# Attention ahead of two MLPs: one of four chunks of p·v as three rounded matmuls, heads 4 to 37

## Chip, cores and metric

One core of one Trainium2 chip. The metric is the device time of one launch in microseconds. The kernel before took 1683.31 us (median of 3 runs, 1678.78 to 1685.2).

## What is computed

Attention over 4 batches of 12 heads (448 tokens, 64 features each), with an RMS norm of q and k ahead of it; then an MLP block with a layer norm; then a second MLP block behind a low-rank mix along the tokens. All of it is 32-bit. The change touches the last product of the attention alone:

```python
q_n, k_n = (rmsnorm(q, g_q), rmsnorm(k, g_k))
scores = scale * np.matmul(q_n, k_n.transpose(0, 1, 3, 2))
scores = scores - np.max(scores, axis=-1, keepdims=True)
attn = np.exp(scores)
attn = attn / (np.sum(attn, axis=-1, keepdims=True) + 1e-09)
return np.matmul(attn, v)
```

## The kernel before

The 48 heads run as a software pipeline; the keys of a head are cut into NC = 4 chunks of CP = 112. In stage i of the loop over heads six generators take turns, one step each per chunk, in the order of `OS`: `sc` (scores of head i and their exp), `mx` (row maxima, head i+2), `pv` (p times v, head i-1), `t1` (transposes of k and q, head i+3), `t2` (transposes of the query's low part, head i+1), `norm` (copying out, head i-2). A stage has four such steps. Beside them run background generators: `pre` (norm of a pair of heads and its split into high and low parts), `pre_v` (load of v for a pair of heads), and from head 14 on the layer norm of the batch that is done (`ln_stats`, `ln_apply`), which works on batch 0 behind head 14 and on batch 1 behind head 26.

What stands in 32 bits is multiplied in two ways. Nearly all products are made from a rounded high part and a low part (type `F32R`, three matmuls). The product p·v alone uses 32-bit operands (`F32`):

```python
if c < NX:
    PE.matmul(po[:, :S], vf[:, j, c, :], ps[c], start=(c == 0), stop=(c == NC - 1))
```

NX is 4, so all chunks go this way, and the branch with `ph, pl` is not used. `vf` holds v in 64 of 128 columns; the others are ones, so that row 64 of the result is the sum of the exponentials.

The order on each engine comes from a scheduler that moves instructions by its own estimate, save those that are pinned to the order of the program. Each engine runs its queue strictly in that order. Names for the steps below: on ScalarE (ACT) L479 is the exp, L303 and L306 round k and q in `pre`, L439 copies the transposed q (`bq`) out of PSUM, L406 issues the load of v. On GpSimd (POOL) L300 scales k and q, L305 and L308 take their low parts, L287 multiplies with the gains, L184 and L219 belong to the layer norm. On VectorE (DVE) L450 takes the maxima and L514 copies the result out. On TensorE (PE) L475 and L476 make the scores, L449 the scores for the maxima, L428, L436 and L463 transpose, L500 is p·v. Seven PSUM banks go round among all these.

Of the kernel before, what the change touches and what calls it, by code (L numbers as in the profile page):

```python
# [8 lines left out]
F32 = mybir.dt.float32  # L9
F32R = mybir.dt.float32r  # L10
# [3 lines left out]
AF = mybir.ActivationFunctionType  # L14
ALU = mybir.AluOpType
AX = mybir.AxisListType

B, H, S, D = 4, 12, 448, 64
P = 128
CP = 112  # L20
NC = S // CP
DM = H * D
DFF = 4 * DM
KD = DM // P
# [6 lines left out]
NWF = 5  # L31
NP0 = 2
EPS = 1e-6
NX = 4
OS = "smpabn"
QW = D + 2
HL = 8
PVY = (0, 1, 2)
# [5 lines left out]
def f32(ap):  # L44
    return ap.bitcast(F32)


def build(tc, qkv, gg, g_ln, w1a, w2a, w1b, w2b, u_in, v_in, out):
    nc = tc.nc
    V, A, PL, PE = nc.vector, nc.scalar, nc.gpsimd, nc.tensor  # L50
    with ExitStack() as es:
# [9 lines left out]
        def bank(name, tag=None):  # L61
            cnt[0] += 1
            tag = tag or banks["tag"]
            return banks["pool"].tile([P, 512], F32, tag=tag, name=f"{name}{cnt[0]}", bufs=banks[tag])
# [40 lines left out]
        v4 = const([4 * R, S], F32R, "v4")  # L105

        def load_ggt(tp):
            gsb = tp.tile([CP, 2, D], F32, tag="gsb", name="gsb")
            nc.scalar.dma_start(gsb, gg)
            ggt = tp.tile([CP, D], F32, tag="ggt", name="ggt")  # L110
            V.scalar_tensor_tensor(ggt, gsb[:, 0, :], 1.0 / D ** 0.5, gsb[:, 1, :], ALU.mult, ALU.mult)
            return ggt
# [29 lines left out]
        def pin(ins):  # L142
            return tc.keep_in_program_order(ins) if pins[0] else ins
# [82 lines left out]
        def attention(ap, ep, ep2, early, late):  # L226
            NH = B * H
            NP = NH // 2
            kks, vfs, vhs, vls, a2s = [], [], [], [], []
            st = {}  # L230
# [13 lines left out]
            pre_load(0)  # L244
            side["ln"] = bank("ln", "ln")
            ggt = load_ggt(ap)
            identr = ap.tile([CP, CP], F32R, tag="identr", name="identr")
            pin(V.tensor_copy(identr, ident[:CP, :CP]))
# [2 lines left out]
                PE.matmul(warm[:, :P], ones_m, ones_m, start=True, stop=True)  # L251
            later = ap.tile([CP, D], F32, tag="later", name="later")
            for i in range(2):
                for lst, nm, dt, one in ((vfs, "vf", F32, 1.0), (vhs, "vh", F32R, 1.0), (vls, "vl", F32R, 0.0)):
                    n = NX if nm == "vf" else NC - NX
                    if n == 0:
                        lst.append(None)
                        continue
                    t = ap.tile([CP, 2, n, P], dt, tag=f"{nm}{i}", name=f"{nm}{i}")
                    PL.memset(f32(t[:, :, :, D:P]), one)  # L260
                    lst.append(t)
            for i in range(NA2):
                t = ap.tile([P, S], F32R, tag=f"a2{i}", name=f"a2{i}")
                PL.memset(f32(t[D:QW, :]), 1.0)
                a2s.append(t)
            qls = []
            for i in range(3):
                t = ep.tile([CP, 2 * NC, QW], F32R, tag=f"ql{i}", name=f"ql{i}")
# [133 lines left out]
            def pre_v(pr):  # L402
                b, hp = divmod(pr, H // 2)
                v = qkv[b, hp, :, 2].rearrange("p (j c) d -> p j c d", j=2)
                for j in range(2):
                    ins = (nc.scalar if pr else nc.sync).dma_start(vfs[pr % 2][:, j, :, 0:D], v[:, j, 0:NX])  # L406
                    if pr:
                        pin(ins)
                if NX == NC:
                    return  # L410
                vr = ap.tile([CP, 2, NC - NX, D], F32, tag="vr", name=f"vr{pr}", bufs=2)
                nc.sync.dma_start(vr, v[:, :, NX:])
                yield
                yield
                yield
                vh, vl = vhs[pr % 2], vls[pr % 2]
                for j in range(2):
                    A.copy(vh[:, j, :, 0:D], vr[:, j])
                yield
                for j in range(2):  # L420
                    PL.tensor_tensor(vl[:, j, :, 0:D], vr[:, j], f32(vh[:, j, :, 0:D]), ALU.subtract)

            def t1(n):
                pr, j = divmod(n, 2)
# [43 lines left out]
            def sc(n):  # L468
                a1, bq, a2 = st.pop(("ab", n))
                t = st.pop(("t2", n))  # L470
                st["p", n] = ps = []
                for c in range(NC):
                    pb = bank("ps")
                    cs = slice(c * CP, (c + 1) * CP)
                    PE.matmul(pb[:CP, :S], a1[:, cs], bq, start=True, stop=False)  # L475
                    PE.matmul(pb[:CP, :S], a2[:QW, cs], t[:QW], start=False, stop=True)  # L476
                    if c < NX:
                        p = ap.tile([CP, S], F32, tag="pf", name=f"p{n}_{c}", bufs=NX + 2)
                        A.activation(p, pb[:CP, :S], AF.Exp)  # L479
                        ps.append(p)  # L480
                    else:
                        p = ap.tile([CP, S], F32, tag="p", name=f"p{n}_{c}", bufs=2)
                        ph = ap.tile([CP, S], F32R, tag="ph", name=f"ph{n}_{c}", bufs=NC - NX + 1)
                        pl = ap.tile([CP, S], F32R, tag="pl", name=f"pl{n}_{c}", bufs=NC - NX + 1)
                        A.activation(p, pb[:CP, :S], AF.Exp)
                        V.tensor_copy(ph, p)
                        PL.tensor_tensor(pl, p, f32(ph), ALU.subtract)
                        ps.append((ph, pl))
                    if c < NC - 1:
                        yield  # L490

            def pv(n):
                pr, j = divmod(n, 2)
                ps = st.pop(("p", n))
                vf, vh, vl = vfs[pr % 2], vhs[pr % 2], vls[pr % 2]
                po = bank("po")
                st["po", n] = po
                for c in range(NC):
                    if c < NX:
                        PE.matmul(po[:, :S], vf[:, j, c, :], ps[c], start=(c == 0), stop=(c == NC - 1))  # L500
                    else:
                        ph, pl = ps[c]
                        PE.matmul(po[:, :S], vh[:, j, c - NX, :], ph, start=(c == 0), stop=False)
                        PE.matmul(po[:, :S], vl[:, j, c - NX, :], ph, start=False, stop=False)
                        PE.matmul(po[:, :S], vh[:, j, c - NX, :], pl, start=False, stop=(c == NC - 1))
                    if c in PVY:
                        yield

            def norm(n):
# [52 lines left out]
            def ORD(i):  # L562
                fs = {"s": (sc, i), "m": (mx, i + MX), "p": (pv, i - 1), "a": (t1, i + T1), "b": (t2, i + T2), "n": (norm, i - NL)}
                return [fs[z] for z in OS]

            for i in range(-3 - T1, NH + 2):
                def ok(n):
                    return 0 <= n < NH
                if i == -3 - T1:
                    start = first_two()  # L570
# [13 lines left out]
                if i - 2 in (H, 2 * H, 3 * H):  # L584
                    b = (i - 2) // H - 1
# [29 lines left out]
        bufs, held, rings, ready = {}, {}, {}, {}  # L615
# [890 lines left out]
```

## Time and profile before

| what | value |
|---|---|
| median of 3 runs | 1683.31 us |
| the profiled execution, its own time | 1675.09 us |
| its span, first to last instruction | 1673.3 us |
| mean granted TensorE clock | 0.997 |
| busy: PE, DVE, ACT, POOL | 99%, 72%, 60%, 63% |
| attention's p·v (L500), first to last start | 28.5 to 338.3 us |

The attention fills the first 340 us, the MLPs the rest. Shares of busy time are means over both. A matmul's duration in the profile runs from its issue to its modelled end and overlaps the ones beside it; what a matmul costs in a row of others is read from the chain of waits, which has one piece behind the other.

### The profile page before, as it was taken

The numbers are of one execution on the slowest core, as the hardware profiler recorded it, in microseconds if no ns is written. First come the engines' busy times: TensorE is split into PE (matmuls) and PEld (weight loads), VectorE is DVE, ScalarE is ACT, GpSimd is POOL, SyncE is SP. The second block draws the span as 40 slices with busy tenths as digits, with TensorE's granted clock in tenths as the row PEclk, the third lists the DMA queues.
The fourth block names the chain that finished last, engine by engine and source line by source line (L and its number), as shares of the span: only waits on it lengthen the run. The fifth ranks groups of instructions, "written<-read, shape, count | busy, mean of one in ns | idle before, by whom it ended". The sixth has DMA issues, their size and how long they took to land.

```text
span 1673.3 us, 24654 instructions
## 1 busy us (share of the span) xinstructions
PE 1661.3 (99%) x8223; PEld 1460.3 (87%) x8223; DVE 1203.5 (72%) x1913; ACT 1000.5 (60%) x2098; POOL 1051.1 (63%) x924
## 2 busy tenths in 40 slices
PE   8999999999999999999999999999999999999999
PEld 6666666689999999999999999999999999999998
DVE  6657777879897887866767686657667854565665
ACT  7877888867878876544544455444445534454541
POOL 5446767559767787755655687555555655776752
PEclk8999999999999999999999999999999999999999
DMA  3435444766755566544445427565657463444432
GB/s 98 117 83 128 121 117 136 205 223 207 236 178 174 185 207 202 190 139 131 152 136 159 157 85 255 190 221 176 226 189 250 166 207 118 147 151 123 150 124 76
DMA packets 134430, 273.39 MB, mean 163 GB/s; under 512 B 37280, under 2 KB 57664, under 8 KB 134304
## 3 DMA queue, kind: packets, MB, share of 16 engines
q1 hardware_dynamic: 112252, 265.24, 49.8%
q10 hardware_dynamic: 22052, 6.59, 1.7%
q8 instruction: 65, 1.06, 0.3%
q14 instruction: 61, 0.50, 0.1%
HBM read 178.80 MB, written 81.96 MB: 156 GB/s over the span
## 4 chain that ended last, share of the span: by engine, by line
PE 94%; DVE 2%; DMA 1%; POOL 1%; issue 1%; ACT 1%; SPq 0%; POOLq 0%; DVEq 0%; ACTq 0%
PE bank L1111 35%; PE bank L1289 33%; PE po L500 7%; PE bank L1233 6%; PE ps L475 2%; PE b L1111 2%; PE pm L449 2%; PE ps L476 2%; PE b L1233 2%; PE t L978 1%; PE pk L428 1%; PE pq L436 1%; PE xt L968 1%; PE pt L463 0%; DMA xl<-rs 0%
## 5 line engine op out<-in xcount | busy, mean ns | idle before, releaser
L1289 PE MATMUL bank<-h,w 128*128 128x448 f32 x2655 | 586.1, 366 | 0.0
L1289 PEld LDWEIGHTS bank<-h,w 128*128 128x128 f32 x2655 | 498.3, 188 | 38.3 <-issue 0.4
L1300 DVE TENSOR_TENSOR x<-x,bank 128x448 f32<-128x448 f32 x450 | 275.8, 616 | 188.8 <-PE bank L1289 183.8
L1111 PE MATMUL bank<-xh,w 128*128 128x448 f32 x1158 | 330.5, 367 | 0.0
L785 POOL TENSOR_TENSOR w<-wf,w 128x384 fp32r<-128x384 f32 x201 | 222.7, 1119 | 133.1 <-ACT w L784 131.6
L785 POOL TENSOR_TENSOR w<-s,w 128x384 fp32r<-128x384 f32 x151 | 173.4, 1151 | 152.4 <-ACT w L784 149.1
L1111 PE MATMUL bank<-T,w 128*128 128x448 f32 x1134 | 251.9, 367 | 0.0
L1111 PEld LDWEIGHTS bank<-xh,w 128*128 128x128 f32 x1158 | 217.2, 188 | 17.5 <-issue 0.7
L1111 PEld LDWEIGHTS bank<-T,w 128*128 128x128 f32 x1134 | 212.3, 188 | 16.4
L1111 PE MATMUL bank<-xl,w 128*128 128x448 f32 x579 | 211.9, 366 | 0.0
L784 ACT CAST w<-s 128x384 fp32r<-128x384 f32 x151 | 77.1, 515 | 174.5 <-PE bank L1111 160.5
L500 PE MATMUL po<-p,vf 112*128 112x448 f32 x384 | 175.6, 539 | 0.2 <-DVE m L450 0.2
L450 DVE TENSOR_REDUCE m<-pm 112x1 f32<-112x448 f32 x192 | 118.5, 619 | 64.4 <-PE pm L449 63.8
L784 ACT CAST w<-wf 128x384 fp32r<-128x384 f32 x201 | 101.5, 514 | 100.6 <-PE bank L1111 81.7
L83 DVE SCALAR_TENSOR_TENSOR wf<-wf,raw 128x384 uint32<-128x384 uint32 x180 | 135.2, 757 | 13.2 <-ACT raw L71 5.3
L785 POOL TENSOR_TENSOR w<-raw,w 128x384 fp32r<-128x384 f32 x72 | 81.9, 1154 | 57.1 <-ACT w L784 57.0
L1111 PEld LDWEIGHTS bank<-xl,w 128*128 128x128 f32 x579 | 108.9, 188 | 8.6
L79 ACT ACTIVATE wf<-raw 128x384 f32<-128x384 f32 x180 | 99.3, 553 | 27.5 <-DMA raw<-in_w2a 11.2
L479 ACT ACTIVATE p<-ps 112x448 f32<-112x448 f32 x192 | 104.5, 546 | 4.3 <-PE ps L476 2.1
L1103 DVE SCALAR_TENSOR_TENSOR h<-tm,h 128x448 fp32r<-128x448 f32 x103 | 99.7, 968 | 2.9 <-ACT h L1102 2.2
L71 ACT ACTIVATE raw<-raw 128x384 uint32<-128x384 uint8 x180 | 100.0, 558 | 0.0
L475 PE MATMUL ps<-bq,a 128*112 128x448 f32 x192 | 98.6, 513 | 0.0
(263 smaller groups left out, 2891.1 us busy)
## 6 DMA issues: line engine op xcount, KB each, us to landing
wd<-wf SPq DMA_DIRECT2D x94, 384.0 KB
ws<-w SPq DMA_DIRECT2D x84, 384.0 KB
w<-ws SPq DMA_DIRECT2D x84, 384.0 KB
wf<-wd SPq DMA_DIRECT2D x51, 384.0 KB
raw<-wd SPq DMA_DIRECT2D x48, 384.0 KB
raw<-in_w1b SPq DMA_DIRECT2D x48, 384.0 KB
raw<-in_w2b SPq DMA_DIRECT2D x48, 384.0 KB
raw<-in_w2a SPq DMA_DIRECT2D x44, 384.0 KB
```

Source lines behind the costliest of these rows:

```text
L71: A.activation(r[:, :, 0], r.bitcast(U8).rearrange("p n (t q) -> p n t q", t=2)[:, :, 0, 3], AF.Copy, scale=1.0 / 32, bias=-31.0 / 64)
L83: V.scalar_tensor_tensor(f, f, 3, r[:, :, 0], ALU.logical_shift_left, ALU.bitwise_or)
L450: V.tensor_reduce(m[:, c:c + 1], pm[:CP, :S], AX.X, ALU.max)
L475: PE.matmul(pb[:CP, :S], a1[:, cs], bq, start=True, stop=False)
L479: A.activation(p, pb[:CP, :S], AF.Exp)
L500: PE.matmul(po[:, :S], vf[:, j, c, :], ps[c], start=(c == 0), stop=(c == NC - 1))
L784: job(A, 520, lambda: A.copy(form(key)[0], src()), ins, ("hi",) + key, [key])
L785: job(PL, 1100, lambda: PL.tensor_tensor(form(key)[1], src(), f32(form(key)[0]), ALU.subtract), [("hi",) + key], key, rel=rel)
L1111: PE.matmul(out[:, :S], wt[:, k, :], xt[:, k, :], start=(first and n == 0), stop=(last and n == 8), skip_group_check=True)
L1233: PE.matmul(at(*to)[:, :S], wt[:, e, :], xt, start=(m in "13" and n == 0), stop=(n == 2), skip_group_check=True)
L1289: PE.matmul(at(*key)[:, :S], wt[:, e % 3, :], t, start=(n == 0), stop=(n == 3 * G - 1))
L1300: V.tensor_tensor(x[b][:, e, :], x[b][:, e, :], at(*key)[:, :S], ALU.add)
```

## The change

For heads 4 to 37 the first chunk of p and of v is split into a rounded high part and a low part, and its product is three `F32R` matmuls in place of one `F32` matmul. It stands last of the four chunks in `pv`. For this VectorE rounds p (a cast), GpSimd subtracts (`part`), and once per pair of heads ScalarE rounds v and GpSimd subtracts (`pre_v`). The parts of p go into tiles that lie idle: those of the layer norm of batch 1 for heads 4 to 23, the weight ring of the MLP for heads 24 to 37. The weights of all p·v matmuls become 66 columns wide in place of 128. The gains are loaded into the last batch's `x` tile.

```diff
-NX = 4
+H0, H2, H1, NV = 4, 0, 38, 1
...
+            def parts(n):
+                return 0 if n < H0 else NV if n < H2 else 1 if n < H1 else 0
...
             def pre_v(pr):
...
+                m = parts(2 * pr)
+                if m == 0:
                     return
...
+                yield
+                yield
+                yield
+                A.copy(vh[:, :, :m, 0:D], vf[:, :, :m, 0:D])
+                yield
+                PL.tensor_tensor(vl[:, :, :m, 0:D], vf[:, :, :m, 0:D], f32(vh[:, :, :m, 0:D]), ALU.subtract)
...
+                def part(c):
+                    ph, pl = homes(n)
+                    V.tensor_copy(ph, ps[c])
+                    PL.tensor_tensor(pl, ps[c], f32(ph), ALU.subtract)
+                    hl.append((ph, pl))
+
                 for c in range(NC):
+                    if 0 <= c - 2 < parts(n):
+                        part(c - 2)
...
             def pv(n):
...
+                m = len(hl)
+                for i in range(NC):
+                    c = (i + m) % NC
+                    if c >= m:
+                        PE.matmul(po[:QW, :S], vf[:, j, c, :], ps[c], start=(i == 0), stop=(i == NC - 1))
                     else:
+                        ph, pl = hl[c]
+                        PE.matmul(po[:QW, :S], vh[:, j, c, :], ph, start=False, stop=False)
+                        PE.matmul(po[:QW, :S], vl[:, j, c, :], ph, start=False, stop=False)
+                        PE.matmul(po[:QW, :S], vh[:, j, c, :], pl, start=False, stop=(i == NC - 1))
```

All told there are 68 more matmuls (two for each of 34 heads), 34 casts on VectorE, 34 + 17 subtractions on GpSimd and 17 copies on ScalarE. The MLPs' instructions stay as they were. Line numbers of `pre` are nine higher in the changed kernel (L300 is L309 there, L305 L314, L308 L317, L287 L296, L303 L312, L281 L290), the exp is L494, `bq` L445.

On PE, the end of p·v of head 4 (`po`), before and with the change; `p_0` to `p_3` are the chunks, `xh` the tile that holds the parts of p:

```order
L500 MATMUL po_953<-p_2_903,vf_349 128x448
L436 MATMUL pq_1008<-identr,qd_839 128x112 x4
L475 MATMUL ps_1018<-bq_742,a_5_699 112x448
L476 MATMUL ps_1018<-t_5_886,a_357 112x448
L449 MATMUL pm_1023<-a_7_859,bq_914 112x448
L500 MATMUL po_953<-p_3_922,vf_349 128x448
L475 MATMUL ps_1031<-bq_824,a_6_781 112x448
```

```order
L509 MATMUL po_964<-p_3_933,vf_348 66x448
L442 MATMUL pq_1021<-identr,qd_847 128x112 x4
L491 MATMUL ps_1032<-bq_749,a_5_706 112x448
L492 MATMUL ps_1032<-t_5_895,a_364 112x448
L455 MATMUL pm_1037<-a_7_868,bq_925 112x448
L512 MATMUL po_964<-xh_87,vh_350 66x448
L513 MATMUL po_964<-xh_87,vl_352 66x448
L514 MATMUL po_964<-xh_87,vh_350 66x448
L491 MATMUL ps_1048<-bq_831,a_6_788 112x448
```

The place of the fourth 32-bit matmul holds three rounded ones; nothing else moves there.

On GpSimd, within the layer norm of batch 0 (`ln_sq`, `ln_d`), before and with the change; `xl<-p` is the new subtraction for p:

```order
L305 TENSOR_TENSOR kk_2181<-raw_1_1804,kk_2181 112x8x64
L184 TENSOR_TENSOR ln_sq_2299<-x_82,ln_mu 128x448
L219 TENSOR_TENSOR ln_d_2646<-x_82,ln_mu 128x448
L308 TENSOR_TENSOR ql_359<-raw_0_1802,qd_2180 112x8x64
L287 TENSOR_TENSOR raw_0_1977<-raw_0_1977,later 112x512
L219 TENSOR_TENSOR ln_d_2552<-x_82,ln_mu 128x448
L300 TENSOR_TENSOR raw_1_1979<-raw_1_1979,sy_2094 112x512
L300 TENSOR_TENSOR raw_0_1977<-raw_0_1977,sy_2094 112x512
```

```order
L314 TENSOR_TENSOR kk_2267<-raw_1_1865,kk_2267 112x8x64
L184 TENSOR_TENSOR ln_sq_2390<-x_82,ln_mu 128x448
L483 TENSOR_TENSOR xl_89<-p_0_2273,xl_89 112x448
L219 TENSOR_TENSOR ln_d_2757<-x_82,ln_mu 128x448
L317 TENSOR_TENSOR ql_366<-raw_0_1863,qd_2266 112x8x64
L296 TENSOR_TENSOR raw_0_2048<-raw_0_2048,later 112x512
L483 TENSOR_TENSOR xl_89<-p_0_2369,xl_89 112x448
L219 TENSOR_TENSOR ln_d_2659<-x_82,ln_mu 128x448
L309 TENSOR_TENSOR raw_1_2050<-raw_1_2050,sy_2175 112x512
L309 TENSOR_TENSOR raw_0_2048<-raw_0_2048,sy_2175 112x512
```

Two subtractions now stand ahead of the scaling of k and q; a third piece, the low part of v (L427), stands four instructions above the first row shown.

On ScalarE, behind the load of v for heads 8 and 9, before and with the change:

```order
L406 DMA vf_349<-in_qkv 112x4x64 x2
L431 CAST a_10_1129<-pk_1124 128x448
L479 ACTIVATE p_1_1140<-ps_1137 112x448
L465 CAST t_8_1151<-pt_1146 66x448
L479 ACTIVATE p_2_1161<-ps_1158 112x448
L439 CAST bq_1172<-pq_1167 128x448
L281 ACTIVATE qsq_1_1175<-raw_1_996 112x512
L479 ACTIVATE p_3_1180<-ps_1177 112x448
```

```order
L416 DMA vf_348<-in_qkv 112x4x64 x2
L437 CAST a_10_1150<-pk_1145 128x448
L494 ACTIVATE p_1_1161<-ps_1158 112x448
L471 CAST t_8_1172<-pt_1167 66x448
L494 ACTIVATE p_2_1184<-ps_1181 112x448
L425 CAST vh_350<-vf_348 112x2x64
L445 CAST bq_1195<-pq_1190 128x448
L290 ACTIVATE qsq_1_1198<-raw_1_1007 112x512
L494 ACTIVATE p_3_1204<-ps_1201 112x448
```

The rounding of v, which needs the load to have landed, stands four instructions behind its issue and ahead of the copy of `bq`.

## Rows read from the trace of the kernel before

**Rows 1.** The page, busy time of each engine, with its share and instructions.
```profile
PE 1661.3 (99%) x8223; PEld 1460.3 (87%) x8223; DVE 1203.5 (72%) x1913; ACT 1000.5 (60%) x2098; POOL 1051.1 (63%) x924
```

**Rows 2.** Busy time in two stretches of 20 us; the first line names the columns.
```profile
core 0: us, PE busy (x) PEld busy (x) DVE busy (x) ACT busy (x) POOL busy (x), PEclk, DMA share, GB/s
75.00:95.00 20.00, 20.00 (x101) 14.03 (x101) 11.54 (x24) 16.09 (x38) 9.38 (x9) 1.00 0.31 77
160.00:180.00 20.00, 20.00 (x99) 13.81 (x98) 14.70 (x30) 17.35 (x43) 16.03 (x15) 1.00 0.41 104
```

**Rows 3.** The chain of waits, last step of a stage: start, length, piece.
```profile
205.76 0.21 PE ps L475
205.97 0.20 PE ps L476
206.17 0.20 PE pm L449
206.38 0.75 PE po L500 x2
```

**Rows 4.** Groups by form, PE, 0 to 700 us: count | busy us, mean ns.
```profile
L500 PE MATMUL po<-p,vf 112*128 112x448 f32 x384 | 175.6, 539 | 0.2 <-DVE m L450 0.2
L449 PE MATMUL pm<-a,bq 128*112 128x448 f32 x192 | 73.4, 383 | 3.0 <-ACT bq L439 2.3 <-DVE u L514 0.5
```

**Rows 5.** Two lines' instructions: count, minimum, median and maximum ns, starts, form.
```profile
L131 DVE CAST v<-f x1: 383/383/383, 60.4 to 60.4; 128x448 fp32r<-128x448 f32 x1
...
L215 POOL TENSOR_TENSOR xl<-ln_d,xh x12: 1127/1144/1177, 191.1 to 285.4; 128x448 fp32r<-128x448 f32 x12
```

**Rows 6.** Groups by form, ACT, 0 to 345 us.
```profile
L303 ACT CAST kk<-raw 112x512 fp32r<-112x512 f32 x22 | 13.6, 616 | 0.0
```

**Rows 7.** Timeline of POOL between layer norms: start, us, instruction [idle before].
```profile
74.19 1.28 POOL L305 TENSOR_TENSOR kk<-raw,kk 112x512 fp32r<-112x512 f32 x1 [3.45 <-ACT kk L303]
76.66 1.28 POOL L308 TENSOR_TENSOR ql<-raw,qd 112x512 fp32r<-112x512 f32 x1 [1.19 <-ACT qd L306]
...
81.58 2.04 POOL L300 TENSOR_TENSOR raw<-raw,sy 112x512 f32<-112x512 f32 x2 [2.38 <-PE pk L428]
```

**Rows 8.** Timeline of POOL in the layer norm of batch 0.
```profile
152.38 1.15 POOL L184 TENSOR_TENSOR ln_acc<-x,ln_mu 128x448 f32<-128x448 f32 x1 [1.70 <-ACT ln_mu L172]
153.48 4.47 POOL L184 TENSOR_TENSOR ln_sq<-x,ln_mu 128x448 f32<-128x448 f32 x4
...
163.81 1.15 POOL L219 TENSOR_TENSOR ln_d<-x,ln_mu 128x448 f32<-128x448 f32 x1
164.92 2.04 POOL L300 TENSOR_TENSOR raw<-raw,sy 112x512 f32<-112x512 f32 x2
...
174.67 2.04 POOL L300 TENSOR_TENSOR raw<-raw,sy 112x512 f32<-112x512 f32 x2 [0.69 <-DVE sy L149]
```

**Rows 9.** Timeline of ACT in the same layer norm.
```profile
166.17 0.61 ACT L303 CAST kk<-raw 112x512 fp32r<-112x512 f32 x1
```

**Rows 10.** Timeline of ACT around a load of v; ACTq issues it.
```profile
67.87 0.50 ACTq L406 DMA_DIRECT2D vf<-in_qkv  x1
...
70.77 0.54 ACT L479 ACTIVATE p<-ps 112x448 f32<-112x448 f32 x1
72.02 0.53 ACT L439 CAST bq<-pq 128x448 fp32r<-128x448 f32 x1 [0.70 <-PE pq L436]
```

**Rows 11.** Timeline of PE, the first matmul that needs that `bq`.
```profile
73.67 0.37 PE L449 MATMUL pm<-a,bq 128*112 128x448 f32 x1
```

**Rows 12.** The chain of waits, transfers on it: start, us to landing.
```profile
124.28 3.50 DMA xl<-rs
...
307.69 5.95 DMA wr<-in_w2a
```

**Rows 13.** Timelines of POOL and of DVE at the same moment.
```profile
221.89 2.12 POOL L308 TENSOR_TENSOR ql<-raw,qd 112x512 fp32r<-112x512 f32 x1 [0.57 <-ACT qd L306]
222.25 0.61 DVE L555 TENSOR_TENSOR x<-x,xl 128x448 f32<-128x448 f32 x1
```

More of the change, by code (lines that the diff above doesn't have):

```diff
@@ L107, in load_ggt @@
         def load_ggt(tp):
-            gsb = tp.tile([CP, 2, D], F32, tag="gsb", name="gsb")
+            gsb = x[B - 1][:CP, 0, :2 * D].rearrange("p (j d) -> p j d", j=2)
             nc.scalar.dma_start(gsb, gg)
@@ L253, in attention, with homes @@
             for i in range(2):
[L254 to L260, printed above, removed]
-                    lst.append(t)
+                for lst, nm, dt, n, one in ((vfs, "vf", F32, NC, 1.0), (vhs, "vh", F32R, NV, 1.0), (vls, "vl", F32R, NV, 0.0)):
+                    t = ap.tile([CP, 2, n, QW], dt, tag=f"{nm}{i}", name=f"{nm}{i}")
+                    PL.memset(f32(t[:, :, :, D:QW]), one)
+                    lst.append(t)
+            spare = [xx[1][:CP, k, :] for xx in (xh, xl) for k in range(KD)]
+            ring_w = [t.rearrange("p a b c -> p (a b c)")[:CP, :S] for t in bufs["w"]]
+            taken = [0]
+            def parts(n):
+                return 0 if n < H0 else NV if n < H2 else 1 if n < H1 else 0
+            def homes(n):
+                pool = spare if n < 2 * H else ring_w
+                i = taken[0] % len(pool)
+                taken[0] += 2
+                return pool[i], pool[i + 1]
             for i in range(NA2):
@@ L404, in pre_v @@
                 v = qkv[b, hp, :, 2].rearrange("p (j c) d -> p j c d", j=2)
+                vf, vh, vl = vfs[pr % 2], vhs[pr % 2], vls[pr % 2]
                 for j in range(2):
-                    ins = (nc.scalar if pr else nc.sync).dma_start(vfs[pr % 2][:, j, :, 0:D], v[:, j, 0:NX])
+                    ins = (nc.scalar if pr else nc.sync).dma_start(vf[:, j, :, 0:D], v[:, j])
                     if pr:
                         pin(ins)
-                if NX == NC:
+                m = parts(2 * pr)
+                if m == 0:
                     return
-                vr = ap.tile([CP, 2, NC - NX, D], F32, tag="vr", name=f"vr{pr}", bufs=2)
-                nc.sync.dma_start(vr, v[:, :, NX:])
                 yield
@@ L415, in pre_v @@
                 yield
-                vh, vl = vhs[pr % 2], vls[pr % 2]
-                for j in range(2):
-                    A.copy(vh[:, j, :, 0:D], vr[:, j])
+                A.copy(vh[:, :, :m, 0:D], vf[:, :, :m, 0:D])
                 yield
-                for j in range(2):
-                    PL.tensor_tensor(vl[:, j, :, 0:D], vr[:, j], f32(vh[:, j, :, 0:D]), ALU.subtract)
+                PL.tensor_tensor(vl[:, :, :m, 0:D], vf[:, :, :m, 0:D], f32(vh[:, :, :m, 0:D]), ALU.subtract)
             def t1(n):
@@ L471, in sc @@
                 st["p", n] = ps = []
+                st["hl", n] = hl = []
+                def part(c):
[3 more added lines that the diff above has]
+                    hl.append((ph, pl))
                 for c in range(NC):
+                    if 0 <= c - 2 < parts(n):
+                        part(c - 2)
                     pb = bank("ps")
@@ L476, in sc @@
                     PE.matmul(pb[:CP, :S], a2[:QW, cs], t[:QW], start=False, stop=True)
[L477 to L488, printed above, removed]
+                    p = ap.tile([CP, S], F32, tag="pf", name=f"p{n}_{c}", bufs=NC + 2)
+                    A.activation(p, pb[:CP, :S], AF.Exp)
+                    ps.append(p)
                     if c < NC - 1:
@@ L493, in pv @@
                 pr, j = divmod(n, 2)
-                ps = st.pop(("p", n))
+                ps, hl = st.pop(("p", n)), st.pop(("hl", n))
                 vf, vh, vl = vfs[pr % 2], vhs[pr % 2], vls[pr % 2]
@@ L497, in pv @@
                 st["po", n] = po
-                for c in range(NC):
-                    if c < NX:
-                        PE.matmul(po[:, :S], vf[:, j, c, :], ps[c], start=(c == 0), stop=(c == NC - 1))
-                    else:
[L502 to L506, printed above, removed]
+                m = len(hl)
[3 more added lines that the diff above has]
+                        PE.matmul(po[:QW, :S], vf[:, j, c, :], ps[c], start=(i == 0), stop=(i == NC - 1))
+                    else:
+                        ph, pl = hl[c]
+                        PE.matmul(po[:QW, :S], vh[:, j, c, :], ph, start=False, stop=False)
+                        PE.matmul(po[:QW, :S], vl[:, j, c, :], ph, start=False, stop=False)
+                        PE.matmul(po[:QW, :S], vh[:, j, c, :], pl, start=False, stop=(i == NC - 1))
+                    if i in PVY:
                         yield
```

## Prediction, made before the changed kernel had run

> **What bounds the kernel now.** I read the page first: PE is busy 99% of the span, the other engines 60 to 72% [rows 1]. Then the busy time by stretches, because a mean over attention and MLPs hides the stage that the change touches. In the attention PE is busy 20.00 of 20 us between the layer norms and inside one. GpSimd goes from 9.38 to 16.03 us and ScalarE from 16.09 to 17.35 [rows 2]. So PE sets the pace, and inside a layer norm two other engines have little room. What a matmul costs I take from the chain of waits, whose pieces follow one another: a rounded matmul takes 0.20 to 0.21 us, the 32-bit product of one chunk (two issues) 0.75 us [rows 3]. The groups' mean durations, 383 and 539 ns, overlap their neighbours and don't serve as prices [rows 4]. Last I read GpSimd's and ScalarE's timelines, where the new work goes.
>
> **TensorE.** Per head one 32-bit product goes (0.75 us) and three rounded matmuls come (3 x 0.205 = 0.61 us): 0.14 us less. For 34 heads that is 34 x 0.14 = **4.8 us less**. At 0.20 us each it would be 34 x 0.15 = 5.1, at 0.21 us 34 x 0.12 = 4.1. PE is on the path throughout the attention, so this counts in full unless something else becomes late. The other 32-bit products keep their 448 columns of p; that their weights shrink from 128 to 66 columns I cost at nothing. What hides it is the stream of p itself: two weight loads per product lie beside 0.75 us of streaming. If a gain were there it could only be part of that 0.75 us, and the trace has no row for it.
>
> **VectorE.** 34 casts of 112x448. The nearest row is the one cast of 128x448, 383 ns [rows 5]: 13 us over 220 us of attention, or 6%. VectorE was busy 14.70 of 20 us even in the layer norm [rows 2]; I cost it at nothing. The cover is its waiting for PE's maxima.
>
> **ScalarE.** 17 copies of 112x128. A copy of 112x512 takes 616 ns [rows 6], so each lies between 0.15 us (a quarter) and 0.62; I take 0.25. The copy of `bq` behind it sat idle for 0.70 us before it began [rows 10], which covers 0.25. The wait inside this copy is a rival below.
>
> **GpSimd.** 34 subtractions of 112x448: the nearest row is 128x448 with 1.14 us [rows 5], and pieces of this size follow each other every 1.1 us (four in 4.47 [rows 8]). The 17 of 112x128 have no row. They lie between nothing and 1.14; by size a quarter of it is 0.3, and I take 0.4. Per pair of heads that is 2 x 1.1 + 0.4 = 2.6 us. Between layer norms GpSimd idles 3.45, 1.19 and 2.38 us in each pair [rows 7], together 7.0: covered, and the low parts of p are wanted only at the end of the next stage.
>
> **Inside a layer norm** the cover is gone. From 152.38 us GpSimd runs without a gap; the next idle time is 0.69 us ahead of 174.67 [rows 8]. In the new order one low part of v and two subtractions stand ahead of the scaling of k that began at 164.92, so it comes 0.4 + 2 x 1.1 = 2.6 us later. It ended its first half at 165.96 (half of 2.04); now 168.5. ScalarE rounds that k at 166.17 [rows 9], 0.2 us behind it, and its queue is strict: it now stands for 2.4 us, with exps and the copy of `bq` behind. How much PE feels I bound by the copy of `bq`: it ended at 72.55, and the matmul that needs it began at 73.67 [rows 10, 11], 1.1 us of room. So of 2.4 us about 1.3 reaches PE. The layer norm of batch 1 has the same pattern, but in its new order only one subtraction stands ahead of the first scaling; I put half there, 0.7 us. Taken: **2.0 us given back**. Below it could be nothing, if banks and queues hold more than I think. Above, some nine heads fall in the three stretches without a gap on GpSimd, of which [rows 8] is the first (22 us, over three stages): 9 x 1.1 + 4.5 x 0.4 = 11.7 us if no part of the lag is absorbed. I take the value near the lower end, because the only slack that a row shows absorbs half of the one stall that I can follow.
>
> **Moved or small.** The gains' load into `x` and the narrower fills with ones lie at the start and change no row on the path. SyncE's queue moves a few issues by one place. The MLPs' instructions are the same and start when the attention ends.
>
> **Sum.** 4.8 less, 2.0 more: 2.8 us less. On the profiled execution, 1675.09 becomes 1672.3. That execution lies 8 us below the median of the runs, so on the median 1683.31 becomes **1680.5**.
>
> **Rivals.**
>
> *Everything is covered* (0.25). For it: between layer norms each wait that I can find has cover. Against it: the 0.2 us between the scaling and the rounding of k in the layer norm. Time: 1683.31 - 4.8 = 1678.5, at best 1678.2.
>
> *The cast and GpSimd's work stop each other* (0.20). In this trace GpSimd's subtraction takes 2.12 us where a `tensor_tensor` of VectorE runs beside it, in place of 1.28 [rows 13, 7]: 0.84 us more. If the new casts do the same, GpSimd loses 34 x 0.84 = 28 us. Between layer norms its 7.0 us of idle time per pair still cover 2.6 + 1.7; in the nine heads inside layer norms it is 7.6 us more of lag. If half reaches PE, as above, 3.8 us go: the sum is 4.8 - 2.0 - 3.8 = 1 us more, 1684.3. The row is of an instruction that reads two tensors and the cast reads one, hence not more than 0.20.
> The Trainium skill (SBUF — State Buffer, "Who interferes with whom") says that VectorE and GpSimd have one pair of ports in common, that a copy or cast in a two-port mode holds it for the whole instruction, and that the other engine is stopped meanwhile; by that rule this rival is the forecast, and the sum 1684.3 instead of 1680.5. The row of 2.12 us agrees with it for an instruction with two inputs; no run here yet shows it for a cast.
>
> *ScalarE waits for the load of v* (0.05). This is the case on the other side. The rounding of v stands four instructions behind the issue of its load. The issue began at 67.87, the exp ahead of the new copy ended at 71.31 [rows 10], 3.4 us later. A transfer of the same 112 KB took 3.50 us from issue to landing, a larger one 5.95 [rows 12]. Up to a landing of 3.4 + 0.7 + 1.1 - 0.25 = 5.0 us PE feels nothing (idle time before `bq`, room behind it, the copy itself). At 5.95 us each pair would cost 1 us: 17 us less the 2.8, 1697. Against it: the row of equal size is well below 5.0.
>
> *Nothing is gained* (0.05). If the durations of the groups were the prices, three times 383 (1149 ns) would replace twice 539 (1078): 34 x 0.07 = 2.4 us more, with the 2.0 given back 1687.7. Against it: the chain of waits.
>
> **Chances and range.** The forecast has 0.42, the rivals 0.25, 0.20, 0.05 and 0.05, and 0.03 is left for what I don't see. A measurement of this kernel can tell about 0.5% from no change, 8.4 us. Only the case of the late load goes beyond it upwards; none goes beyond it downwards, though the runs before differ by 6.4 us among themselves. That makes faster 0.05, same 0.88, slower 0.07. The range goes from 1674 (the best case, 1678, less 4 for the spread of a median) to 1688 (the rival with the ports, 1684.3, plus the same 4); the late load is left out.
>
> **What would show it.** Right: in the chain of waits three pieces of 0.2 us where 0.75 stood; stages between layer norms shorter by 0.14 us; attention's last p·v some 3 us earlier; GpSimd without idle time from 152 to beyond 174 us, and ScalarE idle for about 2 us ahead of the rounding of k near 166 us, released by GpSimd. The ports: the low parts of k and q or the casts with maxima far above 1.28 and 0.38 us. The late load: idle time on ScalarE ahead of the new rounding, released by a DMA, with PE waiting for `bq`. Wrong altogether: a changed time in the MLPs, or PE waiting for the low part of p at the new matmuls.

## The result, and the profile after

The changed kernel took **1696.47 us** (median of 6 runs, 1691.94 to 1702.72), the kernel before 1680.93 (median of 6, 1675.84 to 1685.2): **1.0093 of it, interval 1.0066 to 1.0119**. It is 0.9% slower, where the forecast was no change that can be told (1680.5, with a range to 1688).

The profiled execution took 1692.24 us, its span 1690.5. The page's first part, to be read beside [rows 1]:

```profile
PE 1665.7 (99%) x8257; PEld 1444.7 (85%) x8257; DVE 1229.5 (73%) x1947; ACT 1004.2 (59%) x2115; POOL 1099.1 (65%) x979
```

PE is as full as before, and again this mean says nothing about the stage that matters. Nearly all the loss, 15.5 of the 17.2 us between the two profiled executions, lies in the attention. I follow it by one row that each head has, VectorE's copy-out of p·v (`u<-po`). VectorE's timeline at the copy-out of head 13 and of head 47 (columns: start, duration, line, operation; in brackets idle time before), first before, then after:

```profile
118.61 0.61 DVE L514 COPY u<-po 65x448 f32<-65x448 f32 x1
...
339.57 0.61 DVE L514 COPY u<-po 65x448 f32<-65x448 f32 x1
```

```profile
122.42 0.62 DVE L523 COPY u<-po 65x448 f32<-65x448 f32 x1
...
355.04 0.61 DVE L523 COPY u<-po 65x448 f32<-65x448 f32 x1
```

The differences, 3.81 and 15.47 us, I call the **lag** of a head; the same two rows were read in every run below. From head 47 to the end the two kernels differ by 1.7 us (1333.7 and 1335.4 us), and the runs below show 1333.7 to 1338.5 there, e12 1342.8 (see there). Lag of the changed kernel by head: −0.2 at head 3, +2.8 at 4, +3.8 at 13, +3.5 at 18 (up to here outside the layer norms, mostly), +7.7 at 26, +9.3 at 29, +12.3 at 34, +11.7 at 38, +15.5 at 40 and 47. Three losses stand out: one at the first split heads, steps inside the stretches where GpSimd works on a layer norm, and one at head 40, behind the split heads.

The windows of [rows 2], after (PE, PEld, DVE, ACT, POOL busy, each with its count; granted clock, DMA share, GB/s):

```profile
75.00:95.00 20.00, 18.97 (x98) 12.11 (x97) 13.19 (x25) 15.76 (x37) 12.11 (x12) 1.00 0.30 74
160.00:180.00 20.00, 18.77 (x95) 11.86 (x94) 16.35 (x32) 16.57 (x42) 20.00 (x20) 1.00 0.32 75
```

PE had been busy for the whole 20 us in both; now it lacks 1.0 and 1.2. GpSimd has no gap left in the second. What the three new matmuls take stands in the chain of waits (start, duration of the piece, what it was):

```profile
82.19 0.21 PE po L512
82.39 0.20 PE po L513
82.59 0.20 PE po L514
```

0.61 us stand where 0.75 stood [rows 3]. TensorE's own part of the change came out as forecast.

**The first loss.** The chain at the first split pair with a later load of v, and ScalarE's timeline at both:

```profile
41.49 5.18 DMA vf<-in_qkv
46.75 0.30 ACT vh L425
47.05 0.44 ACT bq L445
47.53 0.46 PE pm L455
...
71.15 4.63 DMA vf<-in_qkv
```

```profile
44.34 0.54 ACT L494 ACTIVATE p<-ps 112x448 f32<-112x448 f32 x1
46.75 0.30 ACT L425 CAST vh<-vf 112x128 fp32r<-112x128 f32 x1 [1.87 <-DMA vf<-in_qkv]
...
75.86 0.30 ACT L425 CAST vh<-vf 112x128 fp32r<-112x128 f32 x1 [2.15 <-DMA vf<-in_qkv]
```

The transfer landed 5.18 us after its issue. ScalarE stood 1.87 us at the rounding of v, `bq` behind it, and PE's maxima behind that. The load issued at 71.15 landed after 4.63 us and was waited for as well, for 2.15 us: ScalarE reached the rounding 2.56 us after the issue there. All places of this line:

```profile
L425 ACT CAST vh<-vf x17: 290/300/310, 46.8 to 270.0; 112x128 fp32r<-112x128 f32 x17
...
  DMA vf<-in_qkv: 12.7, 8
```

Eight of the 17 waited for the load, 12.7 us of idle time in all.

**The later losses.** The casts, by tile (durations: lowest/median/highest in ns):

```profile
L482 DVE CAST w<-p x14: 375/683/1903, 188.0 to 280.7; 112x448 fp32r<-112x448 f32 x14
L482 DVE CAST xh<-p x11: 375/699/1380, 49.7 to 180.7; 112x448 fp32r<-112x448 f32 x11
L482 DVE CAST xl<-p x9: 379/387/944, 70.9 to 166.3; 112x448 fp32r<-112x448 f32 x9
```

The shortest cast takes 375 ns, as [rows 5] let expect; 18 of the 34 took over 500. No cast and no scaling in this trace stands longer than 1.90 us. And this is what a step of the lag looks like: GpSimd's timeline, VectorE's and PE's near 200 us, then three windows with the granted clock.

```profile
194.02 1.14 POOL L483 TENSOR_TENSOR w<-p,w 112x448 fp32r<-112x448 f32 x1 [2.13 <-DVE sy L149]
...
197.22 1.05 POOL L309 TENSOR_TENSOR raw<-raw,sy 112x512 f32<-112x512 f32 x1
198.23 1.14 POOL L219 TENSOR_TENSOR ln_d<-x,ln_mu 128x448 f32<-128x448 f32 x1
```

```profile
199.40 0.68 DVE L222 SCALAR_TENSOR_TENSOR ln_d<-ln_d,gln,ln 128x448 f32<-128x448 f32 x1 [2.62 <-POOL ln_d L219]
```

```profile
200.67 0.45 PE L455 MATMUL pm<-a,bq 128*112 128x448 f32 x1 [1.80 <-DVE m L456]
```

```profile
196.00:200.00 4.00, 2.87 (x15) 1.71 (x13) 1.22 (x2) 4.00 (x12) 4.00 (x5) 1.00 0.67 242
200.00:204.00 4.00, 3.33 (x11) 2.08 (x12) 3.39 (x9) 2.72 (x6) 4.00 (x5) 0.66 0.34 92
204.00:208.00 4.00, 4.00 (x19) 2.38 (x18) 2.48 (x5) 2.42 (x9) 4.00 (x5) 0.92 0.12 29
```

GpSimd, which had itself stood for 2.13 us at a new subtraction until VectorE was ready, is late with a piece of the layer norm. VectorE's queue stands 2.62 us at the instruction that reads it (L222), the maxima behind it are late, and PE stands for 1.80 us. After that the granted clock is at half (1.2 GHz) for a stretch: means of 0.66 and 0.92 over two times 4 us are (0.34 + 0.08) x 4 = 1.7 us of lost clock. PE waits of 1.30 us near 261 and of 1.69 near 313 were followed by the same. In the kernel before, the clock stayed full from 25 us on.

Those two waits have other causes. ScalarE's timeline near 257, and VectorE's at the scaling of the rows of batch 2 (`x<-x,r`), first before, then after:

```profile
257.46 0.62 ACT L312 CAST kk<-raw 112x512 fp32r<-112x512 f32 x1 [2.27 <-POOL raw L309]
```

```profile
295.72 0.62 DVE L555 TENSOR_TENSOR x<-x,r 128x448 f32<-128x448 f32 x1 [1.59 <-DMA r<-rs]
```

```profile
311.34 0.63 DVE L564 TENSOR_TENSOR x<-x,r 128x448 f32<-128x448 f32 x1 [4.53 <-DMA r<-rs]
```

Near 257 the stall that the prediction described comes in the layer norm of batch 1: ScalarE stands at the rounding of k until GpSimd has scaled it, and the exp, the cast that waits for it and the maxima follow late. Near 311 VectorE waits for a load of factors, in the kernel before 1.59 us and now 4.53; the lag goes from +12.8 at head 39 to +15.5 at head 40. In e1, which makes no parts, the same wait is 3.00 us. Why the load comes later was not followed.

### The profile page after: what moved, and what is told of

The parts are those of the page before. It is cut to its first block, busy times and chain, and to the rows that moved or that the text cites. A ratio compares the mean times of both kernels' runs of the same rounds, so it can differ in the third digit from the quotient of the medians.

```text
span 1690.5 us, 24836 instructions
## 1 busy us (share of the span) xinstructions
PE 1665.7 (99%) x8257; PEld 1444.7 (85%) x8257; DVE 1229.5 (73%) x1947; ACT 1004.2 (59%) x2115; POOL 1099.1 (65%) x979
## 4 chain that ended last, share of the span: by engine, by line
PE 87%; DVE 4%; DMA 3%; ACT 2%; POOL 2%; issue 1%; SPq 0%; ACTq 0%; DVEq 0%; POOLq 0%
PE bank L1120 34%; PE bank L1298 32%; PE bank L1242 6%; PE po L509 3%; PE b L1120 2%; PE b L1242 2%; DMA vf<-in_qkv 1%; PE pm L455 1%; DVE m L456 1%; PE ps L491 1%; PE ps L492 1%; DVE ln_xs L163 1%; PE t L987 1%; PE xt L977 1%; ACT p L494 1%
## 5 line engine op out<-in xcount | busy, mean ns | idle before, releaser
L509 PE MATMUL po<-p,vf 112*66 112x448 f32 x316 | 146.8, 547 | 1.7 <-DVE m L456 1.7
L494 ACT ACTIVATE p<-ps 112x448 f32<-112x448 f32 x192 | 105.1, 548 | 7.9 <-PE ps L492 4.2
L1161 DVE TENSOR_TENSOR tm<-tm,bank 128x448 f32<-128x448 f32 x102 | 63.0, 618 | 47.6 <-PE bank L1120 47.0
```

Source lines behind the costliest of these rows:

```text
L509: PE.matmul(po[:QW, :S], vf[:, j, c, :], ps[c], start=(i == 0), stop=(i == NC - 1))
```

## The experiments

Three causes are set against each other, called V, S and Q here. **V**: ScalarE waits for the load of v. **S**: VectorE's casts, or its older instructions, and GpSimd's work stop each other. **Q**: GpSimd is late merely because its queue is longer. V and S were rivals in the prediction, Q was its own step inside the layer norm. The expectations of e2, e4 and e5 call S by P, for ports. The first expectations count from 1681 us for the kernel before; in the rounds of these runs it took 1676.5 to 1677.9.

| run | what differs from the changed kernel | ratio to before (95%) | lag at head 13 / 26 / 47, us |
|---|---|---|---|
| (changed kernel) | | 1.0093 (1.0066 to 1.0119) | +3.8 / +7.7 / +15.5 |
| e1 | no parts made, matmuls alone | 0.998 (0.9966 to 0.9994) | −1.9 / −3.6 / −2.0 |
| e2 | v rounded later | 1.0075 (1.0051 to 1.0099) | −1.3 / +5.3 / +15.5 |
| e4 | no subtraction for p | 1.0099 (1.0065 to 1.0132) | +0.4 / +3.6 / +10.9 |
| e5 | cast with one SBUF operand | 1.0098 (1.0075 to 1.0121) | +0.7 / +8.9 / +15.7 |
| e3 | no cast | 1.0098 (1.0081 to 1.0115) | +2.2 / +11.6 / +18.5 |
| e7 | e2 and e3 | 1.0086 (1.006 to 1.0112) | −0.6 / +1.5 / +8.4 |
| e6 | e2, cast on ScalarE | 1.0075 (1.0054 to 1.0096) | +1.5 / +8.0 / +14.3 |
| e8 | e2, only heads 4–17 and 28–31 | 1.002 (1.0008 to 1.0031) | −0.8 / −0.4 / +0.8 |
| e9 | e2, e5's cast, old instructions moved off the ports | 1.0037 (1.0022 to 1.0051) | −1.8 / +1.3 / +7.6 |
| e10 | old instructions moved, no head split | 1.0014 (1.0 to 1.0027) | 0.0 / −0.7 / +3.7 |
| e11 | e2, e5's cast, heads 4–15 only | 0.999 (0.9977 to 1.0003) | −0.6 / −1.5 / +0.2 |
| e12 | e2, e5's cast | 1.0107 (1.0092 to 1.0123) | −2.0 / +5.2 / +11.9 |

The lag is of one profiled execution each, and at head 3, ahead of every split head, it already lies between −1.0 and +0.9 us. Where it and the ratio part (e7, whose runs go from 1686 to 1699), the ratio counts.

### e1: the matmuls alone

```diff
-                A.copy(vh[:, :, :m, 0:D], vf[:, :, :m, 0:D])
-                PL.tensor_tensor(vl[:, :, :m, 0:D], vf[:, :, :m, 0:D], f32(vh[:, :, :m, 0:D]), ALU.subtract)
...
-                    ph, pl = homes(n)
-                    V.tensor_copy(ph, ps[c])
-                    PL.tensor_tensor(pl, ps[c], f32(ph), ALU.subtract)
+                    ph, pl = still
```

> Leaves out the cast and the subtraction for p and the rounding of v: the three matmuls read parts that are filled once. It measures the TensorE term alone. If three rounded matmuls cost 3 x 0.205 us where 0.75 us stood, and nothing else of the change costs, the time is 1680.9 - 4.8 = 1676. If they are not cheaper: 1681. If the 15 us come from TensorE itself (weights of 66 columns, the new places of the parts): about 1696, as with the whole change.

It took 1674.09 us beside 1677.92, 3.8 us less. From head 3 to 13 the lag goes from −0.59 to −1.87, which is 0.13 us per head, and to head 33 to −4.06; at head 38, behind the last split one, it is −3.68, 0.09 per head for all 34. So the term of 0.14 stands where nothing else is late, and 0.2% of the time is about the most this edit could bring here. The making of the parts costs the rest, some 1.1% (1.0093 − 0.998).

### e2: v rounded later

```diff
-                yield
-                yield
-                yield
-                A.copy(vh[:, :, :m, 0:D], vf[:, :, :m, 0:D])
+                for _ in range(6):
+                    yield
+                pin(A.copy(vh[:, :, :m, 0:D], vf[:, :, :m, 0:D]))
```

> The rounding of v stands some 9 us behind its load in place of 3.5 us, pinned there. Theory V (ScalarE waits for the load of v, 12.7 us of idle time in eight places that the profile shows): these waits go, and with them the 0.3 us or more per pair that are lost outside the layer norms, some 6 to 8 us: 1688 to 1690. Theories Q (GpSimd's queue is late inside the layer norms) and P (cast and subtraction stop each other at the ports): at most 2 us: 1694 to 1697.

No idle time is left ahead of the rounding of v. At head 13 the lag is −1.3 in place of +3.8: **V cost 4 to 5 us by then** (5.1 as it stands, 4.4 if each trace is counted from its head 3). But at head 47 it is +15.5, as without the edit: the layer norms took back what V had given, and the time, 12.8 us above the kernel before, is nearer to what theories Q and P said than to V's. The largest of its stalls, in VectorE's timeline, GpSimd's, PE's, and in windows:

```profile
256.12 4.57 DVE L481 CAST w<-p 112x448 fp32r<-112x448 f32 x1 [1.73 <-ACT p L493]
```

```profile
255.88 2.24 POOL L219 TENSOR_TENSOR ln_d<-x,ln_mu 128x448 f32<-128x448 f32 x2
258.07 1.27 POOL L314 TENSOR_TENSOR kk<-raw,kk 112x512 fp32r<-112x512 f32 x1
259.30 1.14 POOL L219 TENSOR_TENSOR ln_d<-x,ln_mu 128x448 f32<-128x448 f32 x1
260.76 1.13 POOL L482 TENSOR_TENSOR w<-p,w 112x448 fp32r<-112x448 f32 x1 [0.33 <-DVE w L481]
```

```profile
261.86 0.72 PE L454 MATMUL pm<-a,bq 128*112 128x448 f32 x1 [4.70 <-DVE m L455]
```

```profile
258.00:262.00 4.00, 0.14 (x1) 0.14 (x2) 4.00 (x4) 2.66 (x7) 3.67 (x5) 0.52 0.12 29
262.00:266.00 4.00, 4.00 (x10) 2.29 (x10) 3.79 (x8) 1.70 (x6) 3.71 (x4) 0.50 0.13 26
266.00:270.00 4.00, 4.00 (x18) 2.64 (x17) 1.38 (x5) 1.80 (x4) 3.31 (x4) 0.70 0.66 175
```

A cast of 0.38 us lasts 4.57. GpSimd runs four instructions back to back beside it, and the cast ends (260.69) only when GpSimd stops, which it does at 260.44 because its next one needs this very cast. PE stands 4.70 us and then works at half the clock for most of the next 8. That is S, in a form that the prediction did not have: the loser is passed over here not for one instruction but for four, until the other engine has a gap. It isn't always so. In e4 a cast of 2.86 us (196.91) ended while GpSimd's pieces followed each other without a gap, and in the changed kernel no cast stood longer than 1.90. What decides it stays open.

### e4, e5, e3: one half of the pair taken away

e4, then e5 and e3:

```diff
-                    PL.tensor_tensor(pl, ps[c], f32(ph), ALU.subtract)
```

```diff
-                    V.tensor_copy(ph, ps[c])
+                    V.tensor_tensor(ph, ps[c], zero.to_broadcast([CP, S]), ALU.add)
```

```diff
-                    V.tensor_copy(ph, ps[c])
```

In e5 `zero` is a column of zeros in PSUM.

> Leaves out the subtraction for p on GpSimd; the low part is a tile of zeros. Casts, the rounding of v and all matmuls stay. Theory Q: GpSimd is back at about its old load, the losses inside and behind the two layer norms (some 10 us) go: 1686 to 1688. Theory V alone: no change, 1695 to 1697. Theory P: the casts still meet GpSimd's other work, so their mean stays near 0.7 us, and about half of the layer norms' loss stays: 1690 to 1692.

> The cast becomes an addition of p and a zero that lies in PSUM, rounded on the way out: one input from SBUF, about 0.62 us in place of 0.38 us when nothing else runs. Theory P: the long casts (up to 1.9 us) go, all stay near 0.62 us, GpSimd's instructions beside them are no longer stretched, and the time falls by 4 us or more: 1690 to 1692. Theories Q and V: GpSimd has the same queue and VectorE a little more work: 1696 to 1699.

> Leaves out the cast alone: the high part is a tile of zeros, GpSimd subtracts it as before, the rounding of v stays where the change put it. Theory S (a VectorE instruction that shares GpSimd's ports stands until GpSimd has a gap, however many instructions that takes; casts took up to 4.6 us): the stalls behind casts inside the layer norms go; the waits for v (some 4 us) and GpSimd's lag stay: 3 to 8 us above the kernel before. Theory Q (the lag of GpSimd's queue is the cause): 10 to 15 us above it, as with the whole change.

None of the three is measurably better than the changed kernel: 1.0099, 1.0098, 1.0098. They lie 15 to 17 us above the kernel before, so the figures of P and S failed in each; e4 agrees with V's and not with Q's, e5 with Q's and V's, and e3 lies beyond Q's 10 to 15. Without the subtractions (e4) the casts still meet GpSimd's older work; one lasts 5.67 us (VectorE's line, lowest/median/highest):

```profile
L485 DVE CAST w<-p x14: 371/590/5666, 182.2 to 277.2; 112x448 fp32r<-112x448 f32 x14
```

With the operand in PSUM (e5) the cast is a constant 0.61 us whatever GpSimd does, so the ports, and not VectorE's load, stretch the cast:

```profile
L484 DVE TENSOR_TENSOR w<-p,ln x14: 602/610/621, 188.4 to 285.1; 112x448 fp32r<-112x448 f32 x14
```

But the time doesn't fall, because an older instruction becomes the victim. The scaling of batch 1's rows (`ss<-ss,sy`, two SBUF inputs), first before, then in e5:

```profile
L535 DVE SCALAR_TENSOR_TENSOR ss<-ss,sy x5: 178/202/992, 118.5 to 461.8; 128x42 f32<-128x42 f32 x3, 128x28 f32<-128x28 f32 x1, 128x14 f32<-128x14 f32 x1
```

```profile
L546 DVE SCALAR_TENSOR_TENSOR ss<-ss,sy x5: 175/203/5130, 119.8 to 477.8; 128x42 f32<-128x42 f32 x3, 128x28 f32<-128x28 f32 x1, 128x14 f32<-128x14 f32 x1
```

An instruction of 0.2 us stood for 5.13. In e3, where there is no cast at all and so none that GpSimd waits for, it stood for 7.03 us, beside seven GpSimd instructions in a row, and ended at 217.45, when the last of them did (216.11 + 1.28 = 217.39).

### e7 and e6: no cast, or the cast elsewhere, with v rounded later

e7 is e2 and e3 in one; e6 is e2 and

```diff
-                    V.tensor_copy(ph, ps[c])
+                    A.copy(ph, ps[c])
```

> As the one without the cast, and the rounding of v pinned later, so that it finds its load landed. Theories S and V together: both named causes are gone, only GpSimd's lag is left (two stalls of 1 to 2 us); from 1 us below the kernel before to 3 above it. Theory Q: 8 us or more above it.

> Computes all of it, with the rounding of v later and the cast of p on ScalarE (0.55 us per head) in place of VectorE. Theory S: no cast can stand at the ports any more; ScalarE, busy 80 to 87%, takes 9% more: between 2 us below the kernel before and 4 above it. If VectorE's other instructions stand instead, or ScalarE becomes the bound: 6 to 12 us above it.

1.0086 and 1.0075, 14.0 and 12.9 us above the kernel before: taking V and the cast away together still leaves most of the loss. e7 agrees with Q's figure (8 us or more), and e6 lies a little beyond the second of its own (6 to 12). In both, VectorE's square in the layer norm's root (L147) stood for over 3 us near 180 us (3.10 and 3.38), in e6 the scaling as well (3.16). So the cast is one victim among several. That GpSimd's longer unbroken stretch is what makes them stand fits these rows, but no run varied it alone.

### e8 and e11: only heads where GpSimd has gaps

```diff
-                return 0 if n < H0 else NV if n < H2 else 1 if n < H1 else 0
+                return 1 if H0 <= n < 18 or 28 <= n < 32 else 0
```

and e11 with `n < 16` alone and e5's cast.

> Computes all of it, with the rounding of v later, but splits only heads 4 to 17 and 28 to 31, whose casts fall outside the stretches in which GpSimd has no gap. 18 heads x 0.14 us: theory S says 1.5 to 2.5 us below the kernel before, without a cast above 1.5 us and without a fall of the granted clock. If casts cost PE something between layer norms too: no difference or up to 3 us above it.

> Computes all of it: heads 4 to 15 alone are split, all of them ahead of the first layer norm, with the rounding of v later and the cast with its second operand in PSUM. 12 heads x 0.14 us = 1.7 us. Theories S, V and Q together (all losses need a late load, a stand at the ports or a GpSimd without gaps): from 1 to 2.5 us below the kernel before, which is about what five rounds can tell. If it is not below it, the gain per head does not survive even where nothing is full.

With 18 heads the attention ends 0.8 us after that of before, with 12 heads 0.2. No cast of e8 exceeds 1 us, and the clock doesn't fall. e11 gains 1.7 us up to head 39 (12 x 0.14 = 1.7) and loses 1.3 of them at head 40, long behind the split heads, where VectorE waits 2.98 us for `r<-rs` in place of 1.59. Its ratio, 0.999 (0.9977 to 1.0003), can't be told from no change; e8 is 0.2% slower. Both miss the gain that was expected. But of the 5.6 us by which e8's profiled execution is longer, 4.8 lie behind the attention, in the first MLP (see e12), so the 0.2% can't be put down to the split heads.

### e9, e10, e12: the older instructions

e9 has e2's place for v, e5's cast, and in addition

```diff
-                by(V.tensor_tensor(t, y, y, ALU.mult))
+                by(A.activation(t, y, AF.Square))
...
-                y = lpool.tile([P, n], F32, tag="sc", name=f"sy{b}_{h0}", bufs=2)
+                out = y = lpool.tile([P, n], F32, tag="sc", name=f"sy{b}_{h0}", bufs=2)
+                if pool:
+                    y = side["ln"][:, :n]
...
-                V.scalar_tensor_tensor(y, y, 2.0, s, ALU.mult, ALU.subtract)
+                V.scalar_tensor_tensor(out, y, 2.0, s, ALU.mult, ALU.subtract)
```

so that these older instructions have one operand in PSUM or go to ScalarE. e10 has only these two edits, with no head split; e12 is e9 without them.

> Computes all of it, with the rounding of v later, the cast with its second operand in PSUM, and the three old VectorE instructions that stood longest beside GpSimd changed likewise: the square in the layer norm's root goes to ScalarE, the scaling's intermediate lies in PSUM. GpSimd keeps all 51 subtractions. Theory S: no VectorE instruction inside the layer norms stands for over 1.5 us, the granted clock does not fall there, and the time is from 2 us below the kernel before to 3 above it. Theory Q (GpSimd's lag by itself, through waits for its results): 8 us or more above it, with PE or VectorE waiting for GpSimd's results.

> No head is split; only the old VectorE instructions are moved off the ports as in the run before this one, and the weights keep 66 columns. It is the base of that run. All theories: within 2 us of the kernel before, since none of these instructions stood for over 1.0 us there inside the layer norms.

> All 34 heads split, with the rounding of v later and the cast with its second operand in PSUM; the old VectorE instructions stay as they were. With those moved off the ports as well it was 0.37% above the kernel before. Theory S: now they stand beside a GpSimd without gaps (5.1 us once in the run with this cast and the early v): 4 to 9 us more than with them moved, 0.6 to 0.9% above the kernel before. Theory Q alone: the same 0.3 to 0.5%.

e12 against e9 is the closest pair: the same splits, the same casts, and only the old instructions differ, with **1.0107 and 1.0037**. Not all of that is theirs: of the 13.5 us between the two profiled executions 4.4 lie in the attention and 9.1 behind it, 8 of them in the first MLP between 355 and 710 us. There TensorE has no idle time and the full clock, but starts fewer matmuls in the same 50 us, first before, then in e12:

```profile
550.00:600.00 50.00, 50.00 (x247) 46.09 (x246) 42.56 (x62) 39.40 (x75) 35.69 (x31) 1.00 0.59 181
```

```profile
550.00:600.00 50.00, 50.00 (x242) 45.09 (x242) 42.86 (x63) 41.51 (x80) 36.96 (x32) 1.00 0.54 169
```

The same 242 stand there in e5 and e8, and 247 in e2, which has e12's old instructions; no edit explains it, and the cause stays open. The 4.4 us agree with theory S's 4 to 9; the ratio of e12 lies above the 0.6 to 0.9% that it said. VectorE's timeline and GpSimd's in e12, then the same scaling in e9:

```profile
206.02 5.04 DVE L545 SCALAR_TENSOR_TENSOR ss<-ss,sy 128x42 f32<-128x42 f32 x1
```

```profile
206.23 0.43 POOL L428 TENSOR_TENSOR vl<-vf,vh 112x128 fp32r<-112x128 f32 x1
206.62 2.04 POOL L311 TENSOR_TENSOR raw<-raw,sy 112x512 f32<-112x512 f32 x2
208.63 1.14 POOL L484 TENSOR_TENSOR w<-p,w 112x448 fp32r<-112x448 f32 x1
209.73 1.27 POOL L316 TENSOR_TENSOR kk<-raw,kk 112x512 fp32r<-112x512 f32 x1
213.79 1.14 POOL L484 TENSOR_TENSOR w<-p,w 112x448 fp32r<-112x448 f32 x1 [2.78 <-DVE w L483]
```

```profile
L547 DVE SCALAR_TENSOR_TENSOR ss<-ss,ln x2: 186/188/191, 117.4 to 206.3; 128x42 f32<-128x42 f32 x2
```

The scaling stands through GpSimd's pieces and ends at 211.06, when the last of them ends (211.00) and GpSimd has to wait for the next cast, which is queued behind the scaling on VectorE. In e9 it takes 0.19 us. e9 lies 6.7 us above the kernel before, between the figures of S and Q. The largest wait that it still has is Q: PE's timeline, and GpSimd's ahead of it:

```profile
248.03 0.43 PE L515 MATMUL po<-w,vh 112*66 112x448 f32 x1 [1.92 <-POOL w L484]
```

```profile
240.21 5.58 POOL L184 TENSOR_TENSOR ln_sq<-x,ln_mu 128x448 f32<-128x448 f32 x5
245.71 1.17 POOL L219 TENSOR_TENSOR ln_d<-x,ln_mu 128x448 f32<-128x448 f32 x1
246.81 1.16 POOL L484 TENSOR_TENSOR w<-p,w 112x448 fp32r<-112x448 f32 x1
```

The low part of p stood behind six pieces of the layer norm; PE waited 1.92 us for it. Another 2.5 of e9's 7.6 us come at head 40, where VectorE waits 4.11 us for `r<-rs`. e10 shows that moving the old instructions is itself no gain (1.0014, 3.8 us where at most 2 were expected), and that near 290 us the kernel is touchy even without a split: the scaling of batch 2, left in SBUF there, took 1.06 to 1.21 us each time, PE waited 1.96 us and the clock fell.

## Why the prediction was wrong

- **What bounds the kernel, and TensorE's 0.14 us per head: right.** 0.20 to 0.21 us for each of the three matmuls in the chain; 0.13 per head in e1 up to head 13, 0.09 over all 34. The narrower weights at nothing: no run contradicts it.
- **The late load of v, given 0.05: it happened.** The step "a transfer of the same 112 KB took 3.50 us … well below 5.0" failed. The landing was read from a row of another transfer; those of `vf` on the chain landed 4.37 to 5.18 us after their issue. The threshold of 5.0 us failed too: a landing after 4.63 us was waited for and lies on the chain. ScalarE came to the rounding 2.6 to 2.8 us after the issue at six of the eight places, and not 3.4; with these times the prediction's own sum gives 4.1 to 4.3. Eight of 17 loads were waited for. It cost 4 to 5 us by head 13 (e2), less than the 17 of this rival, since half of the loads were in time.
- **VectorE's casts "at nothing": wrong.** The cover was an average (14.70 of 20 us busy [rows 2]); a cast of 0.38 us took up to 1.90 us, and the maxima stand behind it on the same queue.
- **"The cast and GpSimd's work stop each other", given 0.20: right as a mechanism, far too small.** It was priced by one row, 0.84 us more for a GpSimd piece [rows 13]. The runs show the opposite direction: VectorE stands. In the changed kernel that is up to 1.90 us for a cast; in the variants it is 4.57 to 7.03 us, through several pieces, and victims are also instructions that the change doesn't touch (e3, e5, e12). The Trainium skill (SBUF — State Buffer, "SBUF: two separate sides") says that whoever starts first has the shared ports for the whole instruction. That the two exclude each other agrees with these rows, and so does its statement ("Who interferes with whom") that an instruction of VectorE with at most one SBUF input, outside its two-port modes, does not contend with GpSimd, by e5's constant 0.61 us. By a wait for one instruction a cast would have stood 1.1 to 1.3 us; 4.57 us across four doesn't agree with that, and the measurement decides.
- **"2.0 us given back … I take the value near the lower end": the term that failed by most.** From head 18 to 47 the lag grew by 11.9 us (3.5 to 15.5), and with the TensorE gain of heads 19 to 37 (19 x 0.14 = 2.7) some 14.6 were lost, beyond even the upper end of 11.7. Not all of it is GpSimd's: 2.8 us fall at head 40 on the load `r<-rs`, and e1, without any parts, falls 3.2 us short of its gain over the same heads. The stall near 166 us came, in another form: ScalarE idled for 2.07 us there, against the 2.4 forecast, but at an exp, whose buffer of p GpSimd's late subtraction still held; PE felt 0.45 us. The layer norm of batch 1, put at half of that (0.7 us), had the stall as forecast: ScalarE idled for 2.27 us ahead of the rounding of k, PE for 1.30, and heads 33 to 34 lost 2.7. What the sum lacked besides were the victims on VectorE, the load at head 40 and the clock.
- **The clock: not in the prediction.** Three falls of about 1.7 us each, some 5 us, come on top of the stalls that led to them.
- **GpSimd's estimates: right.** 1.14 us per subtraction and 0.43 us undisturbed for the low part of v (estimated 1.1 and 0.4). GpSimd ran from 152.73 us on with one gap of 0.2 us, as forecast.

The causes seem to stand in for each other: no edit of one part alone (e2 to e5) lowers the ratio by more than 0.2%. Of the versions that make the parts for all 34 heads only e9, without V and with the ports free of the casts and of the old instructions of two batches, more than halves the loss. How much of the 15.5 us belongs to each in the changed kernel stays open, since they overlap. It wasn't tried to take the subtractions off GpSimd, or to spread the layer norm's pieces so that GpSimd keeps its gaps; no version here that computes the result beats the kernel before by more than the runs can tell.

## What to carry to other kernels

Where two engines exclude each other at a port, don't price a new instruction by its duration or by one collision: look for the stretches in which the other engine has no gap, and count every instruction, old ones too, that may have to wait for the end of such a stretch. Work added to an engine that has idle time elsewhere may cost far more than it lasts; that closing its last gap is what does it was argued here, not shown. And the landing time of a load is read from the rows of that very load, at several places, before an instruction that needs it is put ahead of others on a strict queue.

## What the runs showed of the hardware

- VectorE's instruction with two SBUF inputs, or its cast from SBUF to SBUF, was passed over for several GpSimd instructions in a row: 4.57 us (e2), 5.04 (e12), 5.13 (e5), 5.67 (e4), 7.03 (e3), for work of 0.2 to 0.4 us. In these five it ended within 0.3 us of GpSimd's stop; in e4 another, of 2.86 us, ended without one. With the second operand in PSUM the same work took 0.19 and 0.61 us beside a busy GpSimd.
- After waits of PE of 1.30, 1.69 and 1.80 us the granted clock was at half for a stretch, about 1.7 us lost each time; after one of 4.70 us most of 8 us ran at half. It doesn't follow every such wait: the clock stayed full after 2.17 us in e12 (211.65) and 1.82 in e6 (185.79).
